# A fused attention and MLP-mixer kernel: the same operations in another written-out order

## The chip, the cores and the metric

The kernel runs on one core of one Trainium2 chip. Its time is the time of one execution on the device in microseconds (us). TensorE (PE) multiplies matrices, VectorE (DVE) and ScalarE (ACT) work on elements and empty the accumulators (PSUM, eight banks of 128 x 512 float32), GpSimd (POOL) and SyncE (SP) issue the transfers, which 16 DMA engines carry out. Each engine takes its instructions strictly in its own order. An instruction that waits holds up all that stand behind it on that engine.

## What is computed

```python
scores = matmul(q, k.transpose(0, 1, 3, 2)) / sqrt(64)     # 8 batches, 12 heads, 448 x 64
x = matmul(maximum(scores, 0) ** 2 / 448, v)               # heads side by side: 448 x 768
h = maximum(x.transpose(0, 2, 1) @ w_tok1, 0) @ w_tok2     # 448 -> 256 -> 448, over tokens
u = x + h.transpose(0, 2, 1)
out = u + maximum(u @ w_ch1, 0) @ w_ch2                    # 768 -> 1536 -> 768, over channels
```

The inputs and the output are float32; the kernel multiplies in bfloat16.

## The kernel before

The work is cut into named pieces of a few instructions. A *stage* is four heads of one batch, so there are 24 stages (s = 0 to 23), three to a batch. The names are these:

- `ldk`, `ldq`, `ldv` s.half (`load`): the loads of a stage, issued by POOL, two transfers of 112 KB each per tensor. They write a ring of four (k, q) or three (v) buffers, so a load waits until the stage that used the buffer is through. `ldf` loads the first q by way of SP.
- `T` and `cp` (`transpose`): for stages 0 to 9 TensorE transposes q and k, and two copies bring them out of PSUM. From stage 10 on (`crossing`), `ik` and `iq` copy k and q on VectorE into one *side buffer* (`NSIDE = 1`), and `xk`, `xq` are transposing transfers on SP's queue from there into `kqT`. The next stage's `ik` waits for this stage's `xk`, `iq` for `xq`.
- `S` s.c (`score`): four matmuls on 64x64 tiles give the scores of one of seven slices c, into two PSUM banks; `r` s.c.e is the relu out of one bank, on ScalarE or VectorE; `q` s.c is the square on VectorE.
- `V` s.c (`value`): the product with v; `xe` brings the finished x out of PSUM.
- `xd` (from stage 5; before that `X` on TensorE and `xc`) is a transposing transfer of x on SP's queue (`mixing`); `t1`, its relu `rt`, `t2` and the sum `u` are the token mixing. `ub` b.g is a transposing transfer of u on SP's queue.
- `C1` b.e (`channel1`) is the first channel product with its relu `c1e`, for batches 0 to 5. For batches 6 and 7 `channel1_pair` forms it from seven half-size products `Q1` to `Q7`, with sums `m`, `y`, evictions `n`, `h` and relus `g`.
- `P1` to `P7` with `a`, `b`, `c`, `f..` (`channel2`): the second channel product, two tiles of 128 tokens at a time, from seven products too, with sums `s1` to `s4` on VectorE. `a`, `b`, `c` and `f21` add the transposed u and so wait for `ub`. `st` stores a tile.
- `wt1`, `wt2`, `wc1`, `wc2` are the loads of weights, `ws` sums of them; `fill:k*n` is n matmuls on bank k whose results nobody reads; `ident` builds the unit matrix for transposing on POOL.

The order is written out in one string, `ORDER`. `Order.run` goes through its words and emits each piece at once. So the string sets the order on every engine and queue together: a word's place decides what stands ahead of it on its engine. Behind the colon stand the PSUM banks of a piece (`S0.6:23`), or the engine: `:A` for ScalarE, `:D` for VectorE. Waits follow from the data, from buffers that are used again and from the banks. `load`, `xd`, `xk`, `xq`, `ub` and `st` are emitted in the same way, so that POOL and SP, too, work through their words in the order of the string.

```python
o = add(Op(f'x{t}{s}', 'SP', emit, [i] + [sc[s - NQ, c] for c in range(KC) if s >= NQ]))
i = raw_last[s, t] = add(Op(f'i{t}{s}', 'DVE', emit, loads[s, t] + [cross.get((s - NSIDE, t))]))
```

Of the kernel before, what the change touches and what calls it, by code (L numbers as in the profile page):

```python
# [66 lines left out]
ldk4.0 fill:1*6 V0.2 S1.5:15 r1.4.1:A q0.5:D V0.3 r1.5.0:A ldq4.0 V0.4 r1.5.1:D S1.2:76 r1.4.0:A V0.5 ldv2.0 q0.6:D
r1.2.1:A r1.2.0:A q1.1:D ldv2.1 fill:1*10 V0.6 T2.0:21 q1.3:D xe0.0:A ldq5.1 S1.0:50 xe0.1:A S1.6:67 cp2.1:D
r1.0.0:A wt1.0 r1.0.1:D cp2.0:A r1.6.1:D ldv3.1 r1.6.0:A q1.0:D fill:3*26 S2.0:34 wt1.1 S2.2:15 q1.2:D S2.3:07
r2.0.0:A V1.0:26 ldk6.0 r2.2.1:A r2.2.0:D r2.3.1:A q1.4:D S2.5:35 ldq6.0 V1.1 r2.3.0:A q1.5:D V1.2 r2.0.1:A ldk5.0  # L70
V1.3 r2.5.1:D r2.5.0:A S2.1:17 T3.0:04 wt2 q1.6:D r2.1.0:A S2.4:53 r2.1.1:A q2.0:D ldk5.1 X0.0:1 cp3.1:A cp3.0:D
# [20 lines left out]
V6.3 S7.2:01 r7.4.0:A r7.4.1:D V6.4 S8.1:42 r7.2.1:A r7.2.0:D V6.5 S7.3:53 V6.6 r8.1.1:A r8.1.0:D t1.5.0:1 r7.3.1:A
r7.3.0:D xe6.0:A xe6.1:D S7.1:02 rt5.0:A S8.2:43 S7.6:56 q7.2:D r7.1.1:A t2.4.0:7 r7.1.0:D r7.6.1:A t2.5.1:1
t2.5.0:2 u4.0:D r7.6.0:A C1.0.1a:0 r8.2.1:A u5.1:D r8.2.0:A u5.0:D V7.0:65 S8.0:73 q7.1:D C1.0.1 r8.0.1:A C1.1.4:1
r8.0.0:D c1e0.1:A q7.3:D q7.4:D S8.3:42 c1e1.4:A V7.1 S7.5:37 r8.3.1:D r8.3.0:A V7.2 T9.0:01 r7.5.1:D r7.5.0:A V7.3
S8.4:24 ldq13.0 cp9.0:A cp9.1:D C1.1.3:3 q7.5:D ldv9.0 r8.4.0:A q7.6:D ldv8.0 r8.4.1:A C1.1.2:7 c1e1.3:D ldq12.0
# [740 lines left out]
```

## Time and profile before

| | us |
|---|---|
| median of three runs (lowest, highest) | 363.33 (359.29, 364.66) |
| profiled execution | 362.15 |
| its span, first to last instruction | 360.3 |
| TensorE busy in it | 343.7 |
| VectorE busy | 317.5 |
| ScalarE busy | 193.7 |
| POOL busy | 92.6 |

The span is what the profile sees; the rest of the execution's time lies around it. The profile has one row per group of instructions (line, engine, tiles out and in, count, busy time, mean of one in nanoseconds), views of who waited for whom, the chain of work that ended last, and sums by stretch of time. TensorE's matmuls overlap and their ends are modelled; how fast they follow one another is seen from the starts of successive groups. PEld is the loading of weights, which runs beside the matmuls. A tile's name stands for all its buffers: `sc_ps` scores, `acc_ps` the product with v, `t_ps` and `h_ps` token mixing, `m_ps` channel products, `x_sb` transposed x, `u_sb` transposed u, `side` the side buffer, `wc` weights.

### The profile page before, as it was taken

What the parts mean: (1) busy time and instruction counts of PE and PEld (TensorE: products, weight loads), DVE (VectorE), ACT (ScalarE), POOL (GpSimd) and SP (SyncE); (2) the same over time, 40 slices, a digit from 0 to 9 for tenths busy, and PEclk for the clock granted to TensorE, in tenths of its full rate; (3) what the DMA queues carried; (4) which work ended last, traced back from release to release, by engine and by line L of the source; (5) the groups of instructions that cost most, each with busy time, mean ns of one, the idle gap of its engine ahead of it and who ended that gap; (6) DMA issues with size and microseconds to landing.
All of it is one profiled execution on the core that took longest, in us unless ns stands there. A gap on an engine that the chain in (4) does not pass through costs nothing.

```text
span 360.3 us, 8771 instructions
## 1 busy us (share of the span) xinstructions
PE 343.7 (95%) x3486; PEld 188.4 (52%) x3486; DVE 317.5 (88%) x621; ACT 193.7 (54%) x406; POOL 92.6 (26%) x157
## 2 busy tenths in 40 slices
PE   6999999999999999897999599999999999999994
PEld 3665455554555554454454256455555565555662
DVE  2999999998999999878999669999999898777983
ACT  3999888867642188570377322858674411453000
POOL 8957246150272130243202500502100000000000
PEclk9899999999999999999999989999999999999999
DMA  8999999989999999997978995798950371253255
GB/s 152 170 148 149 204 202 136 195 117 138 184 166 216 161 125 209 173 155 107 166 136 195 145 127 115 123 168 139 183 115 22 75 147 33 48 119 87 62 137 153
DMA packets 100505, 50.42 MB, mean 140 GB/s; under 512 B 72880, under 2 KB 97136, under 8 KB 100464
## 3 DMA queue, kind: packets, MB, share of 16 engines
q0 software_dynamic: 25904, 21.47, 43.8%
q1 hardware_dynamic: 74240, 28.00, 43.7%
q8 instruction: 27, 0.44, 0.5%
q10 hardware_dynamic: 320, 0.39, 0.3%
q14 instruction: 14, 0.11, 0.1%
HBM read 43.38 MB, written 11.01 MB: 151 GB/s over the span
## 4 chain that ended last, share of the span: by engine, by line
PE 70%; DMA 11%; DVE 10%; SPq 3%; ACT 2%; issue 2%; POOL 2%; DVEq 0%; ACTq 0%; POOLq 0%
PE m_ps L710 21%; PE m_ps L545 18%; PE sc_ps L432 7%; PE acc_ps L456 7%; PE m_ps L617 6%; PE t_ps L500 5%; PE h_ps L509 4%; DVE sq L439 3%; DMA u_sb<-uT_sb 3%; DMA wc<-in_moe_w_ch_dram 3%; DMA x_sb<-xT 3%; SPq L525 2%; DMA kqT<-side 1%; ACT sq L264 1%; DVE out_sb L727 1%
## 5 line engine op out<-in xcount | busy, mean ns | idle before, releaser
L264 ACT ACTIVATE sq<-sc_ps 128x448 bf16<-128x448 f32 x224 | 109.0, 561 | 19.4 <-PE sc_ps L432 18.7
L439 DVE TENSOR_TENSOR sq<-sq 128x896 bf16<-128x896 bf16 x168 | 97.7, 615 | 0.2
L545 PE MATMUL m_ps<-uT_sb,wc 128*128 128x448 bf16 x432 | 89.8, 353 | 0.5 <-DMA wc<-in_moe_w_ch_dram 0.5
L266 DVE TENSOR_SCALAR sq<-sc_ps 128x448 bf16<-128x448 f32 x112 | 65.5, 615 | 4.2 <-PE sc_ps L432 3.7
L264 ACT ACTIVATE r_sb<-m_ps 128x448 bf16<-128x448 f32 (+2 forms) x88 | 40.7, 481 | 47.8 <-PE m_ps L545 46.3
L545 PEld LDWEIGHTS <-wc 128*128 128x128 bf16 x432 | 40.3, 98 | 42.4 <-issue 7.2
L432 PE MATMUL sc_ps<-kqT 64*64 64x448 bf16 x672 | 58.0, 360 | 1.2 <-ACT sq L264 0.3
L456 PE MATMUL acc_ps<-sq,v_raw 64*64 64x448 bf16 x672 | 55.6, 354 | 1.0 <-DVE sq L439 0.9
L286 POOL DMA_DIRECT2D v_raw<-in_v_dram x48 | 29.4, 621 | 85.1 <-PE acc_ps L456 68.8
L710 PEld LDWEIGHTS <-r_sb 128*128 128x128 bf16 x336 | 32.4, 98 | 26.1 <-issue 4.0
L725 DVE TENSOR_TENSOR out_sb<-m_ps,u_sb 128x384 f32<-128x384 f32 x56 | 30.7, 550 | 14.2 <-PE sc_ps L432 6.5
L286 POOL DMA_DIRECT2D kq_raw<-in_q_dram x46 | 28.6, 624 | 56.3 <-DVE side L410 32.9
L264 ACT ACTIVATE r_sb<-t_ps 128x512 bf16<-128x512 f32 (+1 forms) x25 | 14.0, 561 | 42.6 <-PE t_ps L500 42.5
L286 POOL DMA_DIRECT2D kq_raw<-in_k_dram x48 | 29.8, 631 | 19.0 <-DVE side L410 16.0
L710 PEld LDWEIGHTS <-sums 128*128 128x128 bf16 x252 | 24.6, 99 | 18.8 <-issue 3.8
L710 PE MATMUL m_ps<-wc_t,r_sb 128*128 128x384 bf16 x168 | 31.2, 326 | 1.4 <-DVE out_sb L725 1.3
L710 PE MATMUL m_ps<-wc_t,sums 128*128 128x384 bf16 x168 | 31.9, 332 | 0.1
L432 PEld LDWEIGHTS <-kqT 64*64 64x64 bf16 x672 | 21.8, 107 | 18.8 <-issue 11.8
L710 PE MATMUL m_ps<-wc,r_sb 128*128 128x384 bf16 x168 | 30.8, 326 | 0.0
L456 PEld LDWEIGHTS <-v_raw 64*64 64x64 bf16 x672 | 20.0, 106 | 19.5 <-issue 11.6
L500 PE MATMUL t_ps<-x_sb,wt 128*128 128x256 bf16 (+1 forms) x216 | 26.0, 266 | 3.8 <-DMA x_sb<-xT 3.8
L513 DVE TENSOR_TENSOR uT_sb<-h_ps,xT 128x448 bf16<-128x448 f32 x48 | 29.0, 614 | 0.0
(64 smaller groups left out, 322.8 us busy)
## 6 DMA issues: line engine op xcount, KB each, us to landing
out_dram<-out_sb SPq DMA_DIRECT2D x52, 192.0 KB, 3.2
kq_raw<-in_k_dram POOLq DMA_DIRECT2D x48, 112.0 KB, 5.1
v_raw<-in_v_dram POOLq DMA_DIRECT2D x48, 112.0 KB, 5.8
kq_raw<-in_q_dram POOLq DMA_DIRECT2D x46, 112.0 KB, 5.3
wc<-in_moe_w_ch_dram POOLq DMA_DIRECT2D x2, 1152.0 KB, 14.1
wc<-in_moe_w_ch_dram POOLq DMA_DIRECT2D x3, 576.0 KB, 11.9
u_sb<-uT_sb SPq DMA_TRANSPOSE x60, 3.6
sums<-in_moe_w_ch_dram POOLq DMA_DIRECT2D x1, 576.0 KB, 8.1
```

What stands on the lines that cost most here:

```text
L264: nc.scalar.activation(out, ps, AF.Relu)
L266: nc.vector.tensor_scalar(out=out, in0=ps, scalar1=0.0, scalar2=None, op0=ALU.max)
L286: nc.gpsimd.dma_start(out=raws[t][s % NR[t]][64 * half:64 * (half + 1)], in_=src[b, h0:h0 + 2].rearrange('e (p c) d -> p e (c d)', c=KC))
L432: nc.tensor.matmul(o.ps[e][64 * half:64 * (half + 1), :S], lhsT=lhsT, rhs=rhs, start=True, stop=True, skip_group_check=True)
L439: sq_ops[s, c] = [add(Op(f'q{s}.{c}', 'DVE', lambda o: nc.vector.tensor_tensor(out=buf, in0=buf, in1=buf, op=ALU.mult), ev))]
L456: nc.tensor.matmul(o.ps[half][64 * e:64 * (e + 1), :S], lhsT=r[rows, e, c * D:(c + 1) * D], rhs=sq[rows, e, :], start=c == 0, stop=c == KC ...
L500: nc.tensor.matmul(o.ps[:, j, :], lhsT=wt1[:, c, j * 128:(j + 1) * 128], rhs=x_sb[:, p0:p1, c, :], start=c == 0, stop=c == 3)
L513: nc.vector.tensor_tensor(out=uTs[bb % 2][:, 2 * i + a, off:off + S].rearrange('n (c p) -> n c p', c=KC), in0=t2.ps[:, :S].rearrange('n (p ...
L545: nc.tensor.matmul(ps[:, :S], lhsT=wc1[:, g, e * 128:(e + 1) * 128], rhs=uT[:, g, off:off + S], start=g == 0, stop=g == CC - 1)
L617: nc.tensor.matmul(banks[into][:, :S], lhsT=lhs[:, g, k * 128:(k + 1) * 128], rhs=rhs[:, g], start=after is None and g == 0, stop=g == GH ...
L710: nc.tensor.matmul(banks[into][:, :HN], lhsT=lhs[:, e], rhs=wc2[w][:, e], start=after is None and e == 0, stop=e == EH - 1, skip_group_che ...
L725: nc.vector.tensor_tensor(out=out_[:, cols].rearrange('n (g d) -> n g d', d=128), in0=banks[into][:, :HN].rearrange('n (g d) -> n g d', d= ...
```

## The change

`ORDER` is replaced as a whole; nothing else differs. The 1945 pieces are the same ones. Which of them stands ahead of which, the banks, the engine of some evictions, and the filling matmuls (75 in six groups before, 74 in seven after) are new. The new list was made by a planner that played each candidate through with the transfers late at random, and that put relu evictions rather on ScalarE. On ScalarE stand 226 of the 336 relus of scores (224 before), 71 of the 72 of C1 (67), and seven of the eight copies `xc` (two). Of the diff the lines with the words of which the prediction speaks:

```diff
--- before.py
+++ after.py
@@ -59,142 +59,141 @@
 ORDER = """
-ldf.1 ldk0.1 ldf.0 ldk0.0 ldq1.1 ldk1.0 ldk1.1 ldq1.0 cast1.0:A cast1.1:D ldv0.0 ident cast0.0:D cast0.1:A ldv0.1
-T0.1:0 T0.0:1 ldk2.1 cp0.1:A cp0.0:D ldq2.0 fill:2*13 S0.6:23 ldk2.0 S0.4:45 S0.1:67 r0.6.0:A r0.6.1:D S0.0:10
...
-r3.5.0:A X0.1:6 r2.6.0:D r2.6.1:A wc1.1 S3.1:70 t1.0.0:3 xc0.1:D r3.1.1:A q2.6:D X1.0:2 r3.1.0:A ldv4.0 X1.1:5
...
-q3.4:D r4.4.1:A V3.3 S4.5:27 ldq7.1 cp5.0:A cp5.1:D C1.0.9:4 r4.5.0:D ldk7.0 r4.5.1:A q4.0:D C1.0.7:6 wc2.22
...
-r5.3.1:D ldk8.1 r5.5.1:D r5.5.0:A ldq8.1 r5.3.0:A C1.0.2a:7 q5.2:D c1e0.11:A ldv7.0 q5.3:D t1.3.0:0 q5.5:D C1.0.2
...
-ldk9.0 S6.4:13 q6.5:D rt4.0:A S6.0:67 S6.2:05 ldk9.1 r6.4.0:A r6.4.1:D C1.0.0a:2 r6.2.1:A r6.2.0:D wc2.11 C1.0.5:4
...
-ws3.1:D ldk11.1 C1.1.6:1 ub0.2 c1e1.2:A ws3.0:D ldk10.1 ws1.0:D ldv9.1 C1.1.7:0 c1e1.6:A ub0.1 ws1.1:D ldk13.0
...
-r12.3.0:A xe11.1:D st2.0 xe11.0:A q12.0:D S13.1:34 S12.6:02 c1e2.2:A xq14 S13.2:16 q12.3:D t2.9.0:7 r12.6.1:A
...
-r13.3.0:D r13.3.1:A ldk19.0 xk15 r12.4.0:A iq15:D ldk19.1 S13.4:64 q12.4:D c1e2.7:A V13.0:53 ldv14.1 xq15 V12.2
-r13.4.1:D r13.4.0:A V13.1 V12.3 S13.6:72 q13.3:D V12.4 S13.5:64 r13.6.1:A V13.2 ub3.1 r13.6.0:D V12.5 r13.5.1:A
...
-q13.4:D c1e2.8:A q13.5:D S14.0:07 q13.6:D st3.1 V13.4 S14.3:24 r14.0.1:A r14.0.0:D C1.2.1:6 ub2.5 r14.3.1:A a.3:D
...
-r14.2.1:A s3.3:D t1.12.0:4 r14.2.0:A b.4:D r15.1.1:A s4.4:D P5.3:5 rt12.0:A iq16:D s4.3:D P7.3 ldq20.1 xq16 q14.1:D
...
-S17.2:14 r16.6.1:D st9.0 V16.2 S17.5:63 r17.2.1:A q16.5:D V16.3 xd14 S17.4:75 r17.2.0:A V16.4 q16.6:D r17.5.0:A
...
-t1.14.0:2 ldv17.0 a.5:D ldq19.1 P6.6 s2.5:D rt14.0:A xd16 ldv18.1 s3.6:D s3.5:D P6.5 b.6:D s4.5:D S17.0:73 S18.1:15
...
+ldf.0 ldk0.0 ldf.1 ldk0.1 ldv0.0 ldq1.0 ldq1.1 ldk1.1 cast0.0:A cast0.1:D ident ldk3.0 T0.0:0 cast1.0:D cast1.1:A
+ldk1.0 cp0.0:D fill:1*6 T0.1:1 ldv0.1 cp0.1:A ldk2.1 ldk2.0 fill:2*18 S0.6:23 S0.5:45 S0.0:67 r0.6.0:A r0.6.1:D
...
+r2.2.1:D r2.2.0:A ldk6.0 r2.4.0:D r2.4.1:A V2.0:46 ldq5.0 cp3.1:A q2.2:D V2.1 q2.4:D wc1.1 fill:1*6 V2.2 xe1.1:A
...
+t2.1.1:3 r4.5.0:D r4.2.1:A wc1.0 V3.4 u1.1:D r4.2.0:A T5.0:57 q3.5:D S4.3:46 ldq7.0 cp5.1:A C1.0.9:2 cp5.0:D wc2.21
...
+C1.1.10:3 ub0.3 xe7.0:D ldv8.0 r8.1.0:A xe7.1:D wc2.11 r8.1.1:A S8.2:24 ub0.5 q8.0:D S9.2:65 c1e1.10:A C1.1.8:7
...
+ub1.1 r8.6.0:A q9.0:D r9.1.0:A C1.1.7:6 r9.1.1:A q8.6:D rt6.0:A q9.2:D P2.0:7 q9.1:D c1e1.7:A ldv9.1 ws1.1:D V8.0:03
...
+c1e1.4:A q9.4:D xd7 P3.0 c1e1.5:A t2.6.0:7 f12.0:D P4.0 u6.0:D st0.1 iq11:D st0.0 V8.2 V9.0:14 f21.0:D S9.5:26 ub1.0
...
+xe8.0:A xe8.1:D r10.5.1:A s3.1:D xd8 r10.5.0:A V9.6 S10.4:60 a.1:D S10.1:35 xe9.1:A r10.4.1:D t1.7.0:2 r10.4.0:A
+ub1.3 r10.1.1:D r10.1.0:A P6.1 xe9.0:A s2.2:D rt7.0:A s4.1:D xq11 S10.3:40 s3.2:D S10.6:65 S10.2:31 r10.3.1:A
...
+st1.0 t2.7.0:6 iq12:D st1.1 P2.1:5 c.1:D ldq16.1 xq12 u7.0:D P6.2 ldk12.1 f22.1:D ldq14.0 q10.0:D t1.8.0:1 ldv11.1
...
+u8.1:D t2.8.0:6 ik12:D S11.0:14 S11.1:73 u8.0:D ldk16.0 xk12 r11.0.0:A P7.2 r11.1.1:D r11.1.0:A ldq13.1 r11.0.1:A
...
+r12.0.1:A r12.0.0:D xk14 r12.6.1:A xe11.0:D xe11.1:A P2.2:1 q12.0:D c1e2.1:A xd11 q12.2:D S12.5:45 f11.2:D S12.3:26
+S13.0:03 r12.5.1:A r12.5.0:D C1.2.2:7 ub2.0 r13.0.1:A r13.0.0:D r12.3.1:A iq14:D r12.3.0:A C1.2.5:1 ub2.5 c1e2.2:A
+q13.0:D q12.3:D t2.9.1:5 c1e2.5:A xq14 q12.4:D C1.2.8:4 u9.1:D ik15:D V12.0:30 st2.0 c1e2.8:A S13.2:62 q12.5:D V12.1
+st4.1 r13.2.1:A S13.3:71 V12.2 r13.2.0:D S13.1:54 r13.3.1:A st3.0 C1.2.6:2 r13.1.1:D r13.1.0:A xk15 r13.3.0:A
+q13.2:D t1.10.0:6 q13.1:D c1e2.6:A ub2.3 q13.3:D t2.9.0:1 rt10.0:A iq15:D t1.11.0:5 u9.0:D st3.1 q12.6:D V12.3
+rt11.0:A st4.0 V13.0:47 S13.5:26 V12.4 V13.1 st5.1 r13.5.0:D r13.5.1:A S13.4:15 V12.5 V13.2 ik16:D xq15 r13.4.1:A
...
+c1e3.9:A q14.5:D P6.4 q15.2:D f11.3:D P5.3:7 ik17:D b.4:D S14.6:45 f11.4:D ub3.2 P7.3 r14.6.1:A r14.6.0:D q14.6:D
...
+c1e3.7:A xd14 V15.4 q16.5:D S16.1:74 S16.0:26 u12.1:D r16.1.0:A C1.3.10:5 r16.0.1:A r16.0.0:D r16.1.1:A iq18:D
...
+r16.4.0:A st6.0 r16.6.0:D t1.13.0:7 xk18 q16.4:D c1e3.8:A q16.6:D C1.3.5:6 rt13.0:A st6.1 st7.0 t2.12.0:4 c1e3.5:A
...
+ik19:D t1.14.0:6 c1e3.3:A q17.1:D q17.2:D S17.6:57 rt14.0:A V16.6 S17.0:31 r17.6.1:D r17.6.0:A ldv19.1 t2.13.0:4
...
+P7.5 r18.0.1:A b.6:D xk20 r18.0.0:A q18.2:D P7.6 c.5:D xd16 q18.0:D C1.4.3:7 c.6:D f22.6:D P4.5 c1e4.3:A iq20:D
+C1.4.2:4 xq20 f21.5:D ik21:D P3.6 c1e4.2:A P4.6 f12.6:D V17.0:51 f21.6:D S18.3:07 V17.1 r18.3.0:A r18.3.1:D S18.4:34
...
+C1.4.9:2 c1e4.10:A u15.1:D iq21:D P2.6:7 c1e4.9:A P2.5:1 f11.6:D st12.0 V18.2 f11.5:D S19.4:06 xq21 V19.0:42 V18.3
...
+q20.4:D u16.0:D q20.0:D S19.5:35 c1e4.8:A S20.5:70 V19.4 iq22:D r19.5.1:A t2.17.0:6 r19.5.0:D r20.5.1:A t2.16.1:1
+xq22 C1.4.5:5 r20.5.0:A u17.0:D q19.5:D xd18 u16.1:D t2.17.1:3 c1e4.5:A V19.5 ik22:D S20.6:07 S20.1:61 u17.1:D
...
+r21.3.0:A q21.2:D t1.18.0:4 c1e5.5:A q21.3:D ub4.1 q21.4:D V20.4 rt18.0:A S22.0:05 q21.5:D V20.5 ub4.3 S21.1:31
...
+P1.8:2 c1e5.4:A t2.21.0:1 a.8:D V23.5 V22.6 u21.0:D V23.6 xe22.1:A t2.20.0:0 xe22.0:D C1.5.6:7 u20.0:D xd22 xe23.0:A
...
+u21.1:D s3.8:D P6.9 b.8:D s3.9:D P2.9:3 ub7.0 b.9:D s4.8:D P7.8 ub7.1 f11.9:D m1.0:D Q2.0:4 c.8:D t1.22.0:7 st15.1
...
 """
```

More of the change, by code (lines that the diff above doesn't have):

```diff
@@ L67 @@
[L67 to L71, printed above, removed]
@@ L92 @@
[L92 to L96, printed above, removed]
@@ new lines @@
+ldk12.0 r8.2.0:A r8.2.1:D r9.2.0:A ldq10.0 q8.1:D ub0.2 r9.2.1:A C1.1.2:0 ldk11.1 q8.2:D c1e1.8:A ws3.0:D ldq11.1
+ub0.0 S9.0:13 ldk10.0 ws3.1:D c1e1.2:A S8.4:24 S8.3:65 r9.0.0:A C1.1.11:7 ldq11.0 r9.0.1:D r8.4.1:A ub0.4 ldk10.1
+r8.4.0:D r8.3.1:A C1.1.0:0 q8.5:D r8.3.0:A ub1.2 c1e1.11:A q8.4:D q8.3:D S8.6:13 c1e1.0:A S9.1:42 r8.6.1:D t1.6.0:5
+ub1.1 r8.6.0:A q9.0:D r9.1.0:A C1.1.7:6 r9.1.1:A q8.6:D rt6.0:A q9.2:D P2.0:7 q9.1:D c1e1.7:A ldv9.1 ws1.1:D V8.0:03
+S9.3:14 S9.4:25 V8.1 r9.3.0:A ws1.0:D C1.1.1:6 ldv9.0 r9.3.1:A ws2.1:D r9.4.1:A r9.4.0:A ldk11.0 s1.0:D t2.6.1:1
```

214 lines of the change are left out of this document (102 added, 112 removed).

## The prediction

> **What bounds the kernel now.** I begin with the page's head: which engine is full, and how much of the span it leaves.
>
> ```profile
> span 360.3 us, 8771 instructions
> PE 343.7 (95%) x3486; PEld 188.4 (52%) x3486; DVE 317.5 (88%) x621; ACT 193.7 (54%) x406; POOL 92.6 (26%) x157
> ```
>
> TensorE is idle for 360.3 - 343.7 = 16.6 us, VectorE for 43 us, ScalarE for 167 us. An order of the same operations can win TensorE's idle time and whatever stretches its matmuls, and little else. The stretches of nine microseconds show where that time lies (columns: PE, PEld, DVE, ACT, POOL busy, granted clock, DMA share, GB/s).
>
> ```profile
> 0.00:9.00 9.00, 6.18 (x86) 3.50 (x90) 2.10 (x8) 3.35 (x4) 7.88 (x18) 0.93 0.86 152
> 162.00:171.00 9.00, 7.17 (x43) 3.90 (x41) 7.57 (x16) 0.00 (x0) 3.57 (x6) 1.00 0.80 107
> 198.00:207.00 9.00, 5.17 (x37) 2.64 (x36) 6.23 (x13) 3.39 (x9) 4.74 (x9) 0.93 1.35 151
> 207.00:216.00 9.00, 9.00 (x58) 5.08 (x56) 5.27 (x11) 2.61 (x5) 1.02 (x2) 0.88 1.10 128
> ```
>
> Most stretches that are not shown have PE at 9.00 of 9. The first three here lose 2.8, 1.8 and 3.8 us, and after the third the clock is below full. The waits of TensorE and VectorE name the causes (total us, times, longest):
>
> ```profile
> PE t_ps L500 <- DMA x_sb<-xT: 3.8, 1, 3.8
> ...
> PE m_ps L710 <- DVE out_sb L725: 1.3, 1, 1.3
> ...
> PE m_ps L545 <- DMA wc<-in_moe_w_ch_dram: 0.5, 1, 0.5
> ```
> ```profile
> DVE out_sb L725 <- DMA u_sb<-uT_sb: 3.7, 1, 3.7
> ...
> DVE side L410 <- DMA kqT<-side: 2.2, 2, 1.6
> ...
> DVE side L410 <- DMA v_raw<-in_v_dram: 1.0, 1, 1.0
> ```
>
> All of it goes back to late transfers: a transposed x (xd14 before t1.14), a transposed u (ub2.5 before b.4, which holds P7.4), a transposed q (xq14, for which iq15 waits, then a square, then V12.4) and the weights wc1.1 before C1.0.9. The chain of work around the largest:
>
> ```profile
> 193.84 1.32 SPq L414
> ...
> 196.48 9.27 DMA x_sb<-xT
> ...
> 205.80 1.89 PE t_ps L500 x8
> 207.68 2.73 PE m_ps L710 x12
> ```
> ```profile
> 196.05 0.59 POOL L286 DMA_DIRECT2D v_raw<-in_v_dram  x1 [8.46 <-PE acc_ps L456]
> ```
>
> xd14 stands in the list ahead of S17.4, but the queue of SyncE was still at xq18 and reached it at 196.48. POOL, held for 8.46 us, let a batch of loads go at 196.05, and the transpose took 9.27 us. t1.14 then ran at a reduced clock, 1.89 us for 8 matmuls, and the next two products took 2.73 us. For the undisturbed sizes I use these rows of the chain:
>
> ```profile
> 53.44 0.87 PE t_ps L500 x8
> ...
> 226.47 2.27 PE m_ps L545 x12
> 228.74 0.31 PE acc_ps L456 x4
> 229.05 0.19 PE sc_ps L432 x4
> ...
> 232.37 0.38 PE h_ps L509 x2
> ...
> 285.66 1.95 PE m_ps L710 x12
> ```
>
> So the late transpose cost 3.8 of waiting, 1.89 - 0.87 = 1.0 and 2.73 - 1.95 = 0.8 of slow clock: **5.6 us**. The Trainium skill's page "TensorE: Matmul & The Clock Gate" (Part 1, What's actually happening) says that the array falls to half its clock after an idle window of about 3.4 us; the trace agrees, since the wait of 3.8 is followed by 0.88, and the stretch with the wait of 1.3 has 1.00.
>
> **The change part by part.** All operations keep their work; only the list changes, so each part is a matter of distance. I measure a distance in TensorE work that stands between two words of the list, with the rows above: C1 1.14 us, P 0.98, t1 0.87, t2 0.38, S and V 0.19, a change between 64x64 and 128x128 tiles 0.31 - 0.19, about 0.1. In before the places that went wrong stand at 8.7 (xd14 to t1.14), 6.8 (ub2.5 to b.4) and 5.9 us (xq14 to iq15).
>
> *xd14.* In after it stands 10.8 us ahead of t1.14, with five loads in the neighbourhood. This stall goes: -5.6 (bounds -5.6 and 0). But xd22 stands at 7.4, xd18 at 8.2, xd11 at 8.3, xd7 at 8.5 from their t1, nearer than xd14 did. They lie in stretches with fewer loads, so I let one such stall return with a chance of a third: +1.9 (bounds 0 and +5.6).
>
> *ub2.5.* It stands behind C1.2.5 in after, well ahead of b.4. Its successor is ub1.3, 6.4 us ahead of c.1, among four loads and five transposes. One of the three closest u transposes of before (6.7, 6.8 and 6.8) was late, so I count half of the 1.3 us of PE wait as gone: -0.7 (bounds -1.3 and +1.3).
>
> *The single side buffer.* Each ik and iq waits on VectorE for the transpose that last read the side buffer, and behind it on VectorE stand the relu evictions and squares that TensorE needs.
>
> ```profile
> DMA to landing us min/median/max: 2.9/5.1/9.9
> ```
> ```profile
> 145.84 0.62 DVE L410 COPY side<-kq_raw 128x896 bf16<-128x896 bf16 x1 [1.56 <-DMA kqT<-side]
> ...
> 147.04 0.38 PE L456 MATMUL acc_ps<-sq,v_raw 64*64 64x448 bf16 x4 [0.93 <-DVE sq L439]
> ```
> ```profile
> kq_raw<-in_k_dram POOLq DMA_DIRECT2D x48, 112.0 KB, 5.1
> ...
> wc<-in_moe_w_ch_dram POOLq DMA_DIRECT2D x3, 576.0 KB, 11.9
> ```
>
> The first row is for the transposes into kqT (L414), the last two are loads with their median us to landing. After has seven distances under 6 us: xk15 to ik16 3.7 (two t1, one t2, two S, six V), xk20 to ik21 4.2, xq11 to iq12 4.4, xq14 to iq15 4.9, xk18 to ik19 5.1, xq21 to iq22 5.3, xk14 to ik15 5.6; their sum is 33.2. At the median landing of 5.1 VectorE waits 1.4 + 0.9 + 0.7 + 0.2 = 3.2. Two loads are near as well: ldk12.1 stands 4.6 ahead of ik12 (against 5.1: 0.5), and wc2.11 9.5 ahead of ws1.1 (against 11.9: 2.4). Together 6.1; before's own waits, 2.2 + 1.0, go: +2.9 on VectorE. Of 1.56 us there TensorE lost 0.93, so 0.6 of it arrives: **+1.7** (bounds 0, if VectorE catches up, and +20 with all seven at the longest landing: 0.6 x (7 x 9.9 - 33.2) less the waits of before).
>
> *Evictions to ScalarE.* Counted in the two lists, 14 move: two relus of scores, four of C1, five copies of x, one xe, one h, one g.
>
> ```profile
> L266 DVE TENSOR_SCALAR sq<-sc_ps 128x448 bf16<-128x448 f32 x112 | 65.5, 615 | 4.2 <-PE sc_ps L432 3.7
> ```
>
> VectorE loses at most 14 x 0.615 = 8.6 us of its 317.5, ScalarE takes them into its 167 us of idle time. "Rather on ScalarE" is small: the scores' relus go from 224:112 to 226:110. For a square of VectorE TensorE waited only in the 0.93 us above, so most of it lies beside full TensorE work: -1.0 (bounds -8.6 and 0).
>
> *Tile changes.* The TensorE order alternates between 64x64 and 128x128 work 139 times, 129 before: 10 x 0.1 = +1.0 (bounds 0 and +1.2).
>
> *Weights.* wc1.1 stands 14.0 us ahead of C1.0.9 (10.7 before), alone: the 0.5 us of wait go.
>
> *The opening* is written anew. POOL builds the identity after six loads rather than seven, but the second transposition waits for its cast and eighteen filling matmuls stand where thirteen stood: 0 (bounds -2 and +2, from the 2.8 us of idle in the first row of stretches).
>
> **Sum** against the profiled execution: 360.3 - 5.6 + 1.9 - 0.7 + 1.7 - 1.0 + 1.0 - 0.5 = 357.1 us of span. That execution took 362.15, so 1.85 lie around the span: **359.0 us**. The profiled execution stands 1.2 below the median of the three runs, 363.33, and these spread from 359.29 to 364.66, so that about 2% (below 356.1, above 370.6) is what a measurement can tell from no change. My forecast lies 1.2% under the median: within it.
>
> **Rivals.**
>
> *Late transfers lose their hold (faster).* Every distance suffices, nothing returns, and VectorE's relief is worth twice my value: 360.3 - 5.6 - 1.3 - 0.9 - 0.5 - 2.0 + 1.0 = 351.0, so 352.9 us. For it speaks that 3.8 of TensorE's 16.6 us of idle time stand behind one transfer and that u transposes stand further ahead on the whole (half of them over 26 us, 22 before). Against it, the seven short distances. Chance 0.25.
>
> *The side buffer takes over (slower).* One mechanism: the kqT transposes land later than their successors' copies stand away, each copy blocks VectorE, and the scores' banks stay full. With a landing of L at the seven places, TensorE loses 0.6 x (7L - 33.2 + 2.9 - 3.2) on top of 355.4. It passes 368.75 us of span, 2% slower, from L = 8.0; with 8.5 the time is 355.4 + 15.6 + 1.85 = 372.9 us. For it: one landing of 9.9, and transposes of x at 9.27 with loads beside them. Against it: the median of 5.1. Chance 0.15.
>
> *The change doesn't do what it says.* The bytes and the 16 DMA engines are the same; a DMA share of 1.35 in the stretch of that stall says that queues stand behind each other, and moving one transfer away moves another into its place. A stall of xd14's size then comes up elsewhere: 357.1 - 1.9 + 5.6 + 1.85 = 362.7 us. The row for it is the batch of loads at 196.05. The Trainium skill's page "DMA: Bandwidth & Descriptors" (Issuing engines are not separate DMA queues) says that transfers from all issuing engines interleave on the same 16 DMA engines; by that rule this rival is the outcome, and the trace agrees as far as the 9.27 us beside the loads goes. Chance 0.18.
>
> **The numbers.** Forecast 0.42, by itself 356 to 364 us. Faster by over 2% is the first rival, 0.25; slower the second, 0.15; within 2% the forecast and the third, 0.60. The range must reach into the first rival (352.9, less two for the opening) and up to the start of the second: 351 to 371.
>
> **What would show it.** In the waits after: no long wait of t_ps for x_sb, granted clock 1.00 near t1.14; VectorE's L410 waiting some 4 us in total rather than 3.2; PE busy of nearly the same 343 us within a span of 357. I am wrong if TensorE waits for scores' squares for many microseconds (the second rival), or if the opening, costed at nothing, differs from before's by over 2 us when the first C1 begins.

## The result, and the profile after

The changed kernel takes **367.22 us** (median of 19 executions, 364.48 to 372.0), the kernel before 362.99 us (19, 358.36 to 370.8) on the same chip. The ratio is **1.0152 (1.0112 to 1.0192)**. The forecast was 359.0. Executions of one kernel spread by 2 to 4%, disturbed ones left out of the ratios; so one profile says which waits there are, and only the ratio says what they are worth.

The profiled execution took 364.75 us. Line numbers after are one lower than before's (L409 is the side copy). First the head of the page of the changed kernel.

```profile
span 363.0 us, 8769 instructions
PE 344.9 (95%) x3485; PEld 189.6 (52%) x3485; DVE 312.6 (86%) x606; ACT 200.5 (55%) x421; POOL 92.2 (25%) x157
```

VectorE has 4.9 us less to do than before, ScalarE 6.8 more: the evictions moved as counted. TensorE has 1.2 us more busy time, and 18.1 us of idle time instead of 16.6. Its waits in the changed kernel, and VectorE's for the side copies (total us, times, longest):

```profile
PE acc_ps L455 <- DVE sq L438: 5.2, 3, 2.9
PE m_ps L544 <- DVE sq L265: 2.4, 1, 2.4
...
PE sc_ps L431 <- DMA kqT<-side: 1.2, 1, 1.2
PE m_ps L709 <- DVE out_sb L724: 0.9, 1, 0.9
```
```profile
DVE side L409 <- DMA kqT<-side: 8.9, 4, 3.8
...
DVE side L409 <- DMA kq_raw<-in_q_dram: 2.2, 1, 2.2
...
DVE side L409 <- issue: 1.7, 1, 1.7
```

The waits for x, for u and for wc1 that stood at the head of before's tables are gone. In their place stand a square or a relu of VectorE's (7.6 us in two rows, of which 1.2 are V0.1's in the opening), and VectorE itself waited 8.9 us for transposes out of the side buffer, 2.2 in before. The stretches that answer to those shown of before, and one more:

```profile
0.00:9.00 9.00, 6.96 (x89) 3.90 (x89) 2.20 (x8) 3.35 (x4) 7.73 (x18) 1.00 0.85 151
...
156.00:165.00 9.00, 7.82 (x66) 4.15 (x56) 8.50 (x18) 5.50 (x12) 4.79 (x9) 1.00 1.35 136
180.00:189.00 9.00, 6.07 (x77) 4.04 (x80) 8.11 (x16) 3.78 (x9) 5.05 (x9) 0.81 0.96 88
198.00:207.00 9.00, 7.77 (x86) 3.92 (x85) 6.16 (x13) 5.92 (x14) 3.16 (x6) 1.00 1.19 205
```

The loss at 198 to 207 us is 1.2 rather than 3.8. Instead 1.2 are lost at 156 and 2.9 at 180 to 189, with the clock at 0.81 behind a wait of 2.9 us. The pieces of the chain of work around them:

```profile
154.28 8.32 DMA kqT<-side
...
169.87 9.87 DMA kqT<-side
179.86 0.62 DVE side L409
...
182.39 0.63 DVE sq L438
183.06 0.46 PE acc_ps L455 x4
...
200.47 5.32 DMA kqT<-side
...
208.19 1.29 PE m_ps L544 x6
```

xq15 lands after 8.32 us, and S15.2 waits for it (1.2). xq16 lands after 9.87; iq17, which waits for it, holds VectorE, and V14.0 waits 2.9 for a square behind it. xk18 lands after 5.32; ik19 waits, and C1.3.11 stands 2.4 for a relu behind it.

To place the loss I use a number of my own: how late a piece starts against the sum of TensorE work ahead of it in its list (the durations of the prediction). The list after holds 329.2 us of work, before 328.3. What lateness is gained in a part of the list, the parts in us of that work:

```
profile of                  up to 54  54-130  130-180  180-200  200-end
before                          14.1     2.6      4.2      5.8      0.6
after                           15.6     2.1     11.2      0.1      0.5
```

So 7.0 us are lost between 130 and 180 and 5.7 won between 180 and 200. With 1.0 up to 130, 0.9 of work and a tail 0.5 shorter that is 2.6 of the 2.7 us between the spans. The ratio stands for twice as much, 5.5 us (0.0152 x 363): these two executions show half of what the lists differ by, and a single pair of profiles can't place the other half.

### The profile page after: what moved, and what is told of

Its sections match the earlier page's. It is cut to its first block, busy times and chain, and to the rows that moved or that the text cites. A ratio compares the mean times of both kernels' runs of the same rounds, so it can differ in the third digit from the quotient of the medians.

```text
span 363.0 us, 8769 instructions
## 1 busy us (share of the span) xinstructions
PE 344.9 (95%) x3485; PEld 189.6 (52%) x3485; DVE 312.6 (86%) x606; ACT 200.5 (55%) x421; POOL 92.2 (25%) x157
## 4 chain that ended last, share of the span: by engine, by line
PE 76%; DMA 15%; DVE 4%; issue 3%; ACT 1%; POOL 1%; DVEq 0%; POOLq 0%; ACTq 0%
PE m_ps L709 24%; PE m_ps L544 18%; PE acc_ps L455 8%; DMA kqT<-side 7%; PE sc_ps L431 7%; PE m_ps L616 7%; PE t_ps L499 5%; PE h_ps L508 4%; DMA kq_raw<-in_k_dram 3%; DMA x_sb<-xT 3%; DVE sq L438 2%; DMA kq_raw<-in_q_dram 1%; DVE sq L265 1%; PE kqT_ps L390 1%; ACT sq L263 1%
## 5 line engine op out<-in xcount | busy, mean ns | idle before, releaser
L544 PE MATMUL m_ps<-uT_sb,wc 128*128 128x448 bf16 x432 | 91.2, 353 | 2.4 <-DVE sq L265 2.4
L263 ACT ACTIVATE r_sb<-m_ps 128x448 bf16<-128x448 f32 (+2 forms) x95 | 43.3, 481 | 43.3 <-PE m_ps L544 41.4
L455 PE MATMUL acc_ps<-sq,v_raw 64*64 64x448 bf16 x672 | 57.5, 368 | 5.7 <-DVE sq L438 5.2
L431 PE MATMUL sc_ps<-kqT 64*64 64x448 bf16 x672 | 59.0, 363 | 2.3 <-DMA kqT<-side 1.2
L455 PEld LDWEIGHTS <-v_raw 64*64 64x64 bf16 x672 | 21.7, 109 | 22.6 <-issue 15.9
L431 PEld LDWEIGHTS <-kqT 64*64 64x64 bf16 x672 | 22.7, 107 | 20.7 <-issue 12.5
L709 PE MATMUL m_ps<-wc_t,sums 128*128 128x384 bf16 x168 | 30.9, 326 | 0.9 <-DVE out_sb L724 0.9
L409 DVE COPY side<-kq_raw 128x896 bf16<-128x896 bf16 x28 | 17.1, 612 | 12.9 <-DMA kqT<-side 8.9
L726 DVE TENSOR_TENSOR out_sb<-m_ps,out_sb 128x384 f32<-128x384 f32 x42 | 23.1, 553 | 5.0 <-PE m_ps L709 4.8
```

Source lines behind the costliest of these rows:

```text
L263: nc.scalar.activation(out, ps, AF.Relu)
L431: nc.tensor.matmul(o.ps[e][64 * half:64 * (half + 1), :S], lhsT=lhsT, rhs=rhs, start=True, stop=True, skip_group_check=True)
L455: nc.tensor.matmul(o.ps[half][64 * e:64 * (e + 1), :S], lhsT=r[rows, e, c * D:(c + 1) * D], rhs=sq[rows, e, :], start=c == 0, stop=c == KC ...
L544: nc.tensor.matmul(ps[:, :S], lhsT=wc1[:, g, e * 128:(e + 1) * 128], rhs=uT[:, g, off:off + S], start=g == 0, stop=g == CC - 1)
L709: nc.tensor.matmul(banks[into][:, :HN], lhsT=lhs[:, e], rhs=wc2[w][:, e], start=after is None and e == 0, stop=e == EH - 1, skip_group_che ...
L726: nc.vector.tensor_tensor(out=out_[:, cols], in0=banks[into][:, :HN], in1=out_[:, cols], op=ALU.add)
```

## The experiments

Theories A, B and C of the first runs: A, loads wait at the head of POOL's queue and go in a pile, in which transposes land late; B, the opening; C, a loss spread over the list. D is the side buffer by itself; E to H come up on the way.

### Where in the list

Five lists change over from one order to the other. Up to the word shown they are one list, and the words that are left follow as the other has them.

```diff
 e1: ... r5.5.1:D ldq8.1 r5.5.0:A          (after's, to 54 us)
+    wc2.22 c1e0.7:A q5.4:D xe4.1:A ...    (rest as before)
 e2: ... iq14:D r12.3.0:A C1.2.5:1         (after's, to 143 us)
+    ldq16.0 ub2.3 st4.0 t2.9.1:4 ...      (rest as before)
 e3: ... P7.7 q23.1:D u19.0:D              (after's, to 277 us)
+    C1.5.6:6 c1e5.6:A C1.5.4:2 ...        (rest as before)
 e7: ... c1e2.6:A q13.0:D st2.1            (before's, to 143 us)
+    ldq16.1 c1e2.11:A ldk17.1 ...         (rest as after)
 e11: ... xe4.0:D c1e0.10:A ldv6.0         (before's, to 54 us)
+    wc2.21 xc3.0:A q5.1:D ...             (rest as after)
```

> The list of after up to r5.5.0 (343 words, 54 us of its profile), then the list of before for what is left. Theory A (the pile-up: in after the loads wait behind one at the head of POOL's queue and go in batches at 154, 181 and 205 us, the transposes then land after 8 to 13 us, and the single side buffer holds VectorE): no batch of this kind here, so the time of before, ratio 0.997 to 1.004 (the opening alone is 1.3 us later in the two profiles). Theory B (the opening: too many evictions and fills early): most of the 5.5 us of the ratio 1.015 are here, ratio 1.010 to 1.018. Theory C (the loss is spread over the whole list, a little in each part): about a seventh of it, 1.002.

> The list of after up to C1.2.5 (874 words, 143 us of its profile), then that of before. Theory A: still ahead of the first batch (154 us), so 0.997 to 1.005. Theory B: 1.010 to 1.018, as with the opening alone. Theory C: two fifths of the loss, about 1.006.

> The list of after up to u19.0 (1618 words, 277 us of its profile), then that of before. Theory A: all three batches are in it, so the full loss, 1.012 to 1.019, and VectorE's copies to the side buffer wait 8 us or more for transposes. Theory B: the same 1.010 to 1.018, but without need of those waits. Theory C: about 1.012.

> The list of before up to its word st2.1 (143 us), then the words that are left in after's order: the converse of the run with after's list up to 143 us. Theory D: after's short distances, all but two of which come behind 143 us (iq15, ik16, iq16, iq17, ik19, ik21, iq22), cost what they cost in after: 366 to 368. If the loss arises ahead of 143 us, as the converse run says on its face (1.019 with after's first part alone), this one gives before's time, 362 to 364. If it is the seam between two lists that cost in that run, this one is slower than both, 368 to 371.

> Before's list up to its word ldv6.0 (54 us), then the rest in after's order: the converse of the run with after's opening. TensorE stood behind its work by 13.9 to 19.2 us at that place in the five profiles with after's opening and by 12.5 to 14.1 in the three with before's. If the opening costs (theory B): 2 us less than after, 365 (364 to 366), still slower than before. If it costs nothing, as the run with after's opening says by its ratio (0.9988), 366.5 to 368. If the whole loss of after's list arises ahead of 54 us in the way its loads then stand: 361 to 363.

Measured against before, each on the chip of its own run: e1 **0.9988** (0.9924 to 1.0053), e2 1.0193 (1.0138 to 1.0248), e3 1.012 (1.0046 to 1.0195), e7 **0.9926** (0.9868 to 0.9984), e11 1.0172 (1.0047 to 1.0298).

The opening is not the loss: after's costs nothing that shows with before's rest (e1, at most 0.5%), and before's does not help after's rest (e11). B falls. After's last 220 us are no loss either: behind before's first 143 us they are faster than before's own (e7). What costs needs after's order from 54 to 143 us. e2 has that and loses, but its seam puts words out of place, and it loses in other waits than after does. The lateness of after grows from 130 to 180 us, so what stands shortly ahead of 143 is suspect.

### The loads

e4 moves every load of the stages from 10 on directly behind the piece that frees its buffer; e9 moves eight of the thirteen that stand behind 134 us.

```diff
 e4:
-... ik16:D xq15 r13.4.1:A S13.6:62 V12.6 r13.4.0:A q13.5:D V13.3 ldk20.0
+... ik16:D ldk20.0 ldk20.1 xq15 r13.4.1:A S13.6:62
 e9:
+V11.5 ldq16.0 ... C1.2.1:7 ldq17.0 ... C1.2.2:7 ldv14.0 ... t2.9.0:1 ldq18.0
```

> The list of after with only POOL's words moved: each load of stages 10 to 23 stands directly behind the piece that frees its buffer, so that no load waits long at the head of the queue and no batch of eight builds up. Theory A with the batches as its cause: the transposes land within 7 us, VectorE's copies to the side buffer wait under 4 us instead of 12.9, and the time falls to before's or below, ratio 0.990 to 1.004. If the transposes pile up on SP's queue by themselves, without the loads: waits stay over 8 us and the ratio stays 1.010 to 1.019. Theories B and C: 1.010 to 1.019 too.

> After's list with eight loads (ldq16.0, ldq17.0, ldq17.1, ldk17.0, ldq18.0, ldq18.1, ldv14.0, ldv14.1) moved out of the thirteen behind 134.3 us of TensorE work into the stretch from 120 to 131 that has none, 1.6 us apart; their buffers are free there. Nothing else is moved. Theory F (the bunch of loads holds the transposes): the transposes issued between 145 and 165 us land at a median of 5 to 7 us rather than 10.4, the loss between 130 and 180 falls from 9 us to 4 to 5: 362.5 to 364.5. Theory E (the stores): landing stays at 9 to 11, 366 to 368. If both are needed, each alone brings 1 to 2 us.

e4 has the highest median of all lists, 374.69 us against 362.99, but no interval: its executions spread from 364.15 to 385.34, and the fastest is no slower than after's fastest, 364.48. The waits of e4, in an execution of 375.12: VectorE waits longer for the side buffer, and now for weights too.

```profile
DVE side L409 <- DMA kqT<-side: 12.3, 5, 4.7
DVE wc_t L328 <- DMA wc<-in_moe_w_ch_dram: 5.2, 1, 5.2
```

That loads wait at the head of POOL's queue is thus not the whole harm: theory A had under 4 us for this wait. That loads collide earlier when they are sent as soon as they may is my reading; no run shows it apart. e9 has 1.0001 (0.9883 to 1.0119): the value that F had, but the interval takes in that of E too. In its profile the transposes issued between 145 and 165 us landed at a median of 6.3 us, as F had it; the lateness gained between 130 and 180 is still 7.9, and xq15 still landed after 8.05 us with five of the thirteen loads left behind it. So the pile of loads does not decide that landing; what it costs elsewhere stays open. xd11, now beside moved loads, took 7.7 us instead of 3.2.

### The side buffer by itself

```diff
-NSIDE = 1
+NSIDE = 2
-wc2 = {... for w in ('11', '21', '22', 't1', 't2', 't3', 't4')}
+wc2 = {... for w in ('11', '21', '22', 't1', 't2', 't3')}
+wc2['t4'] = wc2['t3']
```

> The changed kernel with its own list and two side buffers rather than one, so that ik and iq of a stage wait for the transposes of the stage before the last. The room comes from letting the weights t4 stand on top of t3 (ws4 writes over t3 before P7 reads it), which changes the numbers of the fourth and seventh product and no instruction's size. Theory D (the single side buffer is the loss): VectorE's waits for kqT<-side, 8.9 us in the profile of after, go to nearly 0; at 0.6 of TensorE time per microsecond of VectorE's, as in before, 5.3 us come back: 367.2 - 5.3 = 361.9, so 360 to 363.5, no slower than before. Theory C (the loss is spread over the list: late transposes that TensorE itself waits for, evictions in another place): the waits of kqT<-side go, others take their place, 365.5 to 368.

> The kernel before with the same two side buffers and the same shared weights, as the control of the run with after's list. Its waits for kqT<-side are 2.2 us in one profile, so theory D gives 363.0 - 0.6 x 2.2 = 361.7 (360 to 363), and with two side buffers the two lists within 0.3% of one another. Theory C: 362 to 363.5, and after's list stays 1.0 to 1.5% behind.

After's list with two buffers: 1.0103 (1.0027 to 1.0179); before's: 1.0014 (0.9922 to 1.0106). VectorE's wait for kqT<-side is gone from e5's table, and yet, by the ratios, a third of the loss went (by the interval, anything from none to four fifths). Theory D had at most 363.5 us, a ratio of 1.0014, which the interval leaves out. TensorE's first row in e5 says why:

```profile
PE sc_ps L432 <- DMA kqT<-side: 6.3, 1, 6.3
```

S15.2 waits for xq15 itself, which landed after 11.2 us. The buffer is one of the places where a late transpose hurts; the lateness is the thing. D falls as the whole cause.

### The stores

Three stores stand directly ahead of xq15 on SyncE's queue in after. Issues of SyncE in after (start, us, what), and the landing of the two transposes behind the stores:

```profile
152.31 1.87 SPq L758 DMA_DIRECT2D out_dram<-out_sb  x3
154.28 2.92 SPq L413 DMA_TRANSPOSE kqT<-side  x2
157.25 3.14 SPq L524 DMA_TRANSPOSE u_sb<-uT_sb  x2
160.71 4.19 SPq L478 DMA_TRANSPOSE x_sb<-xT  x1
```
```profile
L413 SPq DMA_TRANSPOSE kqT<-side x2: 1332/1406/1479, 154.3 to 155.7; - x2
...
DMA to landing us min/median/max: 8.3/9.4/10.4
```

e8 moves six stores forward; e10 does so together with e9's loads; e12 only puts three behind xk16; e16 is e8 again; e15 bunches six in before's list.

```diff
 e8, e16:
-... ik15:D V12.0:30 st2.0 ... V12.1 st4.1 ... st3.0 ... xk15 ... st3.1 ... st4.0 ... st5.1 ... ik16:D xq15
+... ub2.2 st3.0 ... xk13 st3.1 ... ub2.1 st2.0 ... xd10 st5.1 ... ub2.0 st4.1 ... xq14 st4.0 ... xk15 ... xq15
 e12:
-... st3.1 ... st4.0 ... st5.1 ... ik16:D xq15 ... xk16
+... ik16:D xq15 ... xk16 st3.1 st4.0 st5.1
 e15 (before's list):
+ldk19.0 st4.1 st2.0 st2.1 xk15 ... u10.1:D st3.0 st5.1 st3.1 xd12
```

> After's list with six stores moved forward on SyncE's queue: st2.0, st3.0, st3.1, st4.0, st4.1 and st5.1 stand between 127.8 and 133.1 us of TensorE work there, right ahead of the transposes xq15, xk16, ub3.0 and xd13; here they stand between 108 and 126. Under after's list the transposes issued between 145 and 165 us landed at a median of 10.4, 10.6 and 11.2 us (three profiles), under before's list or before's first 143 us at 4.0 to 5.5. Theory E (the stores hold the transposes): their landing falls to 5 to 7 us, TensorE's loss between 130 and 180 us of its work from 9 us (mean of 11.2, 7.0, 9.4) to 4 to 5: 362.5 to 364.5. Theory F (the loads do it: none between 118.3 and 134.3 us of the list, then thirteen within ten): landing stays at 9 to 11 us, 366 to 368.

> After's list with the six stores and the eight loads moved as in the two runs before this one. Theories E and F together: transposes issued between 145 and 165 us land at 4 to 6 us as under before's list, and what is left against before is the opening (1 to 2 us) less the stall of xd14 that after's list does not have (4 to 5): 361 to 363. If neither holds: 366 to 368.

> After's list with one thing moved: the stores st3.1, st4.0 and st5.1 stand behind xq15 and xk16 on SyncE's queue rather than directly ahead of them. The bytes in that neighbourhood stay the same, the thirteen loads stay in their bunch. In the profiles with the stores ahead xq15 landed after 8.3, 7.0, 11.2, 8.1 and 7.9 us (after, and four others), xk16 after 8 to 15; with them far ahead after 3.0 and 3.0. Theory G (order on the queue: each store takes SyncE 0.63 us to issue, so xq15 and xk16 start with the loads instead of before them): xq15 lands in 3 to 4 us, xk16 in under 6, the time falls to 361 to 364.5, ratio to before 0.995 to 1.004. Theory H (the bytes of the stores): xq15 and xk16 gain at most 1 or 2 us, ub3.0 and xd13 stay at 10 to 13, 365.5 to 368, ratio 1.01 to 1.02.

> The converse: before's list with six stores put where after's list has its own, st4.1, st2.0 and st2.1 directly ahead of xk15, and st3.0, st5.1 and st3.1 directly ahead of xd12 (at 129.2 and 133.4 us of TensorE work; before has them between 120.9 and 134.6). Seven loads follow at 138 to 141. In before the transposes xk15, xq15, ub3.1, xd12 and ub2.5 landed after 6.7, 6.4, 3.4, 4.1 and 7.1 us, and the loss of TensorE between 130 and 180 us of its work is 4.3, 1.5 and 1.1 us in three profiles with before's list. If the place of the stores is what costs, in any list: the landing of xd12 and ub2.5 grows to 8 us or more, and the time by 4 to 6 us: ratio 1.010 to 1.017. If stores cost only where thirteen loads follow at once, as in after's list: no change, 0.995 to 1.004.

> The same kernel as the run with after's six stores spread (0.9912 from four executions, 0.9807 to 1.0016), for a narrower interval. If that result holds: 0.985 to 0.999. If it was chance: 1.008 or more.

Measured: e8 **0.9912** (0.9807 to 1.0016), e16 **1.0079** (1.0026 to 1.0133), e10 1.0127 (1.0018 to 1.0236), e12 1.0108 (1.0042 to 1.0174), e15 0.9908 (0.9838 to 0.9978).

In e10 the two edits do not add. xq15 lands after 3.0, but xk14, now among the moved loads, after 11.4 instead of 4.7, and VectorE waits up to 7.3 us for it in e10:

```profile
DVE side L409 <- DMA kqT<-side: 10.7, 2, 7.3
```

The landing of xq15 and xk16 is settled. e8, SyncE's queue and the landing of xq15 and xk16:

```profile
155.39 2.59 SPq L413 DMA_TRANSPOSE kqT<-side  x2
158.03 2.54 SPq L524 DMA_TRANSPOSE u_sb<-uT_sb  x2
```
```profile
L413 SPq DMA_TRANSPOSE kqT<-side x2: 1237/1242/1247, 155.4 to 156.7; - x2
...
DMA to landing us min/median/max: 3.0/3.8/4.6
```

The profiles of after's neighbourhood fall into two groups without overlap:

```
                                    xq15 lands after (us)          xk16
stores ahead (after e3 e5 e9 e11 e17)   8.3 7.0 11.2 8.1 7.9 7.2     8.1 to 14.6
stores away (e8 e10 e12 e13 e16 e18)    3.0 3.0  2.9 3.0 3.0 3.1     4.4 to 5.5
```

Between them lies e4, with the stores ahead and other loads behind: 5.9, and xk16 6.9. In e7 and e14 one store, st3.1, stands directly ahead of xq15 and eleven of the thirteen loads in a bunch behind it: 3.4 and 3.3, and xk16 4.3 and 4.4. So the bunch of loads alone does not make xq15 late.

What it is worth in time is less settled. Between 130 and 180 us of the list the lateness gained is 11.2, 7.0, 9.4, 7.9, 9.9 and 3.6 with the stores in that stretch (after, e3, e5, e9, e12, e17), 3.5, 3.0, 7.1 and 5.0 with the stores spread (e8, e13, e16, e18), and 4.2, 1.1 and 1.5 with before's order there (before, e1, e6); e10 and e11, profiled in executions of 372.73 and 374.22, are not among them. The means are 8.2, 4.7 and 2.3: over half of what after loses there, though the first two groups overlap. e8 and e16 are one kernel, and their intervals just miss each other; e16, from three times as many executions, came out where its expectation had chance for e8. Weighted by their widths the two give 1.0045, which would put about 0.011 of 0.0152 down to the stores; e16 alone puts 0.007, and its interval overlaps after's. So it is shown that these landings hang on the place of the stores; that the time falls with them is likely, not shown.

Part of the gain is given back. In all four profiles with the stores spread SyncE reached xq14 only 4.7 to 4.8 us after TensorE had passed its place in the list (1.5 in after). iq15 waited 1.6 to 2.3 us for it (1.0 in after), and S13.4, which needs an operation of VectorE behind iq15, cost TensorE 1.5 to 2.2 us, which it does not in after. Where SyncE has this much to issue, a store that makes room for one transpose can hold up another. This is read from the profiles; no run tests it.

e12 tells order from bytes. Here the three stores go directly behind xk16; rows of e12:

```profile
153.39 2.71 SPq L413 DMA_TRANSPOSE kqT<-side  x2
156.15 1.87 SPq L758 DMA_DIRECT2D out_dram<-out_sb  x3
158.06 3.98 SPq L524 DMA_TRANSPOSE u_sb<-uT_sb  x2
```
```profile
DMA to landing us min/median/max: 2.9/3.7/4.4
```

xq15 and xk16 land early, as theory G says, but the time stays at 1.0108, as H says. Transfers issued between 145 and 165 us, median landing in after, e8 and e12 in turn:

```profile
v_raw<-in_v_dram POOLq DMA_DIRECT2D x4, 112.0 KB, 9.4
...
x_sb<-xT SPq DMA_TRANSPOSE x2, 12.9
```
```profile
v_raw<-in_v_dram POOLq DMA_DIRECT2D x4, 112.0 KB, 6.1
...
x_sb<-xT SPq DMA_TRANSPOSE x3, 8.7
```
```profile
v_raw<-in_v_dram POOLq DMA_DIRECT2D x5, 112.0 KB, 9.1
...
x_sb<-xT SPq DMA_TRANSPOSE x1, 13.0
```

With the stores behind xk16 the loads and xd13 are as late as in after. The order on the queue decides who is late; that somebody is late goes, as far as e8 and e12 tell, with the 576 KB more in this stretch (e8 moves three further stores as well). The Trainium skill's page "DMA: Bandwidth & Descriptors" (Issuing engines are not separate DMA queues) says that the time a sequencer takes to start a transfer is usually small against the transfer. The trace differs here: a store holds SyncE for 0.62 us (three for 1.87) of a median of 3.5 to its landing, and a transpose for 1.24 of the 3.0 us after which xq15 landed in e8.

e15 shows the limit. In before's list bunched stores make xd12 land after 8.5 us (4.1 before) and ub2.5 after 8.9 (7.1), as the first theory had it. Yet the list is not slower: 0.9908 refutes that theory's 1.010 to 1.017 and lies below the second's 0.995, which its interval still reaches. So a late transpose need not cost anything; that it costs only where something near waits for it, and that a moved store frees another place, is my reading.

### One short distance

ik19 is moved later, in after's list alone (e17), with the stores spread (e13, e18), and in e7's list (e14).

```diff
-... r17.5.1:D ik19:D t1.14.0:6 ... q17.5:D c1e3.11:A P1.5:3 xk19
+... r17.5.1:D t1.14.0:6 ... q17.5:D ik19:D c1e3.11:A P1.5:3 xk19
```

> The list with the six stores spread, and ik19 5.1 us of TensorE work later, from 5.1 to 10.2 us behind xk18, for whose landing it waited (2.8 us in after, 2.5 in the run with before's first 143 us), which C1.3.11 paid with 2.4 and 2.1 us of TensorE time. It also repeats the verdict on the stores. If the stores are the larger part of after's loss: ratio to before 0.985 to 0.998, 357 to 362. If the last result on the stores was chance: 1.005 to 1.015.

> Before's list up to st2.1 (143 us), then after's order, with ik19 10.2 instead of 5.1 us behind xk18. The run without this edit had 0.9926 (0.9868 to 0.9984) and lost 2.5 us at C1.3.11. If the wait of ik19 is what C1.3.11 pays: C1.3.11 loses under 0.5 us, 2 us less than that run: ratio 0.985 to 0.99. If another operation on VectorE takes its place: 0.99 to 0.995.

> After's list with ik19 alone moved, from 5.1 to 10.2 us of TensorE work behind xk18; the stores stay where after has them. C1.3.11 waited 2.4 us for VectorE in after, 2.1, 4.2 and 3.1 in three other profiles with ik19 at 5.1, and in no profile with ik19 at 10.2. Theory D in part (this one distance of the side buffer is 2 to 3 us of after's loss): C1.3.11 loses nothing, 1.0152 becomes 1.006 to 1.010. If another wait takes its place (xd15 ahead of t1.15, 1.0 and 4.5 us in the two profiles with ik19 late): 1.011 to 1.018.

> Both edits of after's list again (0.9895, 0.9817 to 0.9972, in six executions), on the same chip as ik19 alone. If the two add: about as much below the stores alone (1.0079 and 0.9912 in two runs) as ik19 alone lies below after, 0.993 to 1.001. If the first run was luck: 1.004 or more. If it holds: 0.984 to 0.995, faster than before's list too.

Measured: e13 0.9895 (0.9817 to 0.9972), e18 1.0008 (0.9956 to 1.006), e14 **0.9876** (0.9796 to 0.9956). For e17 there is no interval: its six executions spread from 356.67 to 372.44, median 365.64 against 361.33. TensorE's waits, first in e7, then in e14:

```profile
PE m_ps L544 <- DVE sq L265: 2.1, 1, 2.1
...
PE t_ps L499 <- DMA x_sb<-xT: 1.1, 2, 0.6
```
```profile
PE t_ps L499 <- DMA x_sb<-xT: 3.0, 3, 1.5
```

The wait of C1.3.11 is gone in all four kernels. It is absent in e3, e5 and e8 too, with ik19 at 5.1, but there ik19 itself waited 0.2 us or not at all; and where ik19 waited, C1.3.11 waited 0.4 us less (2.84 and 2.42 in after, 2.52 and 2.09 in e7, 3.49 and 3.07 in e16, 4.67 and 4.24 in e12). So ik19 was its cause. 1.9 us more for transposed x stand in e14's table in its place. e14 is no measurable gain on e7, since the intervals overlap; whether ik19 adds to the stores is open too (e13 and e18 weighted: 0.997, stores alone 1.0045). Together the two edits take after's list back to before's time.

The lists that beat both kernels are e7 and e14: 359.61 and 359.42 us, 0.7 and 1.2% below before. e15's interval lies below 1 as well, though its edit was meant to cost; that of e13 does too, but its repetition e18 did not bear it out.

## Why the prediction was wrong

**xd14.** Right. Before's order gains 5.8, 4.5 and 6.0 us of lateness between 180 and 200 (before, e1, e6), after 0.1: -5.7 for -5.6.

**A stall that returns.** No x transpose stalled TensorE in after's profile. Stalls of that kind did come back, through the side buffer, and in sum larger than xd14's: 1.1 (V13.4) + 1.2 (S15.2) + 2.9 (V14.0) + 2.4 (C1.3.11) = 7.6 us.

**ub2.5 and wc1.1.** Right: neither a wait of out_sb for u_sb nor one for wc is left. Of ub2.5's 1.3 us I had counted half.

**The single side buffer.** Here the forecast failed. I had 6.1 us of VectorE waits and +1.7 on TensorE; the trace has 8.9 + 2.2 + 1.7 = 12.8 of idle time at the copies, and TensorE waited 6.5 us for squares and relus behind them (0.9 before) and 1.2 for xq15 itself. Three things were wrong in that step:

- The landing. I took 5.1, the median of the whole of before's run. Where the copies stand close, between 145 and 165 us, after's nine transposes have a median of 10.4, and before's six had 5.3. A bunch of stores in after's list stood ahead of them, and I had not looked at where the stores stand at all; xq15 to S15.2, 7.9 us in the list, I had not measured either.
- The selection. The largest wait, 3.8 us, is at xq16 to iq17, 10.1 us of work apart and so not among my seven. Of the seven, three waited: iq15 1.0, ik16 1.3, ik19 2.8. A load at a distance of 5.4 (ldq13.1 to iq13) cost 2.2 and was not listed.
- The start. I compared the landing with the distance, as if SyncE issued a transpose when TensorE passes its place. SyncE issues one transfer after the other and was behind, as these rows of after show for xk18 and ik19 (SyncE, TensorE, VectorE):

```profile
196.63 1.83 SPq L413 DMA_TRANSPOSE kqT<-side  x1
198.50 1.88 SPq L758 DMA_DIRECT2D out_dram<-out_sb  x2
200.47 1.41 SPq L413 DMA_TRANSPOSE kqT<-side  x1
```
```profile
197.72 1.30 PE L544 MATMUL m_ps<-uT_sb,wc 128*128 128x448 bf16 x6
...
203.18 1.04 PE L499 MATMUL t_ps<-x_sb,wt 128*128 128x256 bf16 x8
```
```profile
205.91 0.62 DVE L409 COPY side<-kq_raw 128x896 bf16<-128x896 bf16 x1 [2.84 <-DMA kqT<-side]
```

In the list xk18 stands ahead of C1.3.5, the first row of TensorE, and ik19 ahead of t1.14, the second: 5.46 us apart on TensorE, and xk18 landed in 5.32. But xk18 was issued only 2.75 us after TensorE had begun C1.3.5, since SyncE was busy with xq18 and two stores (st8.0, st6.0). It landed at 205.79, and VectorE, free from 203.07, waited 2.84 us. In the same way xq16 was issued 3.7 us behind TensorE; its landing of 9.87 is shorter than its distance of 10.1, and yet iq17 waited 3.8.

My second rival had the right mechanism with the wrong condition: it was to decide from a mean landing of 8.0 us at the seven places. There the mean was 4.0; the late ones were others. The third rival, that a stall of the same size comes up elsewhere, describes the profile best, and its 362.7 was still 4.5 short. The first rival, with every distance sufficing, is refuted.

**Evictions.** VectorE lost 4.9 us of work, of at most 8.6. That brought nothing visible: TensorE's waits for VectorE rose, since squares stand behind copies that wait for transfers, not behind work.

**Tile changes.** Not measured apart: the list holds 0.9 us more work by the prediction's own durations, and TensorE's busy time rose by 1.2.

**The opening.** Right at 0 within its bounds of 2: 1.5 us later at 54 us in the profile (where V0.1 alone waits 1.2), no loss in e1.

By the sum: 357.1 us of span forecast, 363.0 measured. Every gain that I counted came, except that of VectorE's relief. What was too small is the side buffer's +1.7: the 7.6 us above, with the direct wait for xq15, exceed it by 5.9, the whole difference between forecast and trace. VectorE's relief that did not come (1.0) and the opening (1.5) weigh about as much as the x stall that did not return (1.9) and the other half of ub2.5 (0.6). The executions on the whole lose more than this profile shows, and where is not known.

**Open.** Why e17's one profile, with stores ahead and xq15 at 7.2 us, gains only 3.6 us of lateness between 130 and 180; and the rest of the loss, about 0.4% (1.6 us) with the stores spread, for which the new wait of S13.4 would have the size.

## What to carry to other kernels

A median landing time is no price for a transfer: look at the landing in the stretch where its reader waits, with everything that stands near it on all queues, stores too. When work is reordered, list for each engine what comes to stand directly ahead of the transfers with the least room, and count that room from when the transfer's queue gets to issue it, not from when the busiest engine passes its place. And try the halves of a new order apart: here one half was worth having and the other was not.

## What was not expected of the hardware

- A transposing transfer of 128 x 896 (xq15) landed in 2.9 to 3.1 us in six profiles and in 7.0 to 11.2 in six others. What tells the two groups apart is three stores of 192 KB directly ahead of it; the thirteen loads behind it are in place in five of the six in either group.
- Loads sent as early as their buffers allowed did not help: that list has the highest median here, 374.69 us against 362.99 before and 367.22 after, though its executions spread too far for an interval.
- The length of one wait does not tell whether the granted clock falls. In after it fell behind a wait of 2.93 us (V14.0, the first two rows) and stayed at 1.00 around one of 2.42 (C1.3.11, the third). In e7 it fell behind one of 2.09 (C1.3.11, the fourth row), and in e5 it stayed behind one of 3.15 (t1.15, the fifth; same columns as above):

```profile
183.00:184.00 1.00, 0.94 (x13) 0.64 (x16) 1.00 (x4) 0.04 (x1) 1.00 (x3) 0.62 1.32 156
184.00:185.00 1.00, 1.00 (x16) 0.73 (x12) 0.88 (x3) 0.74 (x2) 0.93 (x2) 0.50 0.85 51
...
207.00:216.00 9.00, 7.80 (x55) 4.46 (x55) 9.00 (x20) 4.64 (x11) 2.78 (x5) 1.00 1.23 159
```
```profile
201.00:202.00 1.00, 1.00 (x4) 0.44 (x3) 1.00 (x3) 0.54 (x1) 0.89 (x2) 0.50 1.56 114
```
```profile
215.00:216.00 1.00, 1.00 (x10) 0.75 (x9) 0.00 (x0) 0.26 (x1) 0.00 (x0) 1.00 1.39 152
```

The Trainium skill's page "TensorE: Matmul & The Clock Gate" (Part 1, What's actually happening) gives an idle window of about 3.4 us; the trace differs, as far as the modelled ends of matmuls allow, with falls to half behind 2.93 and 2.09 us. That the trace agrees with it, as the prediction has it, holds for the two waits named there and not for these.
